# K transposed head by head: 8 transposes a step for 12, and copies that move between partition halves

## The chip, the cores and the metric

The kernel runs on one core of a Trainium2 chip. Its engines are TensorE (PE; its weight loads are listed as PEld), VectorE (DVE), ScalarE (ACT), GpSimd (POOL) and SyncE (SP), which here issues most DMAs. The metric is the device time of one execution in microseconds, the median of three runs.

## The reference

Linear attention with decay over blocks, and then a mixture of experts that takes for each token the two best of 8 by noisy gates. The change is in the first part, of which this is the core (4 batches, 8 heads, 768 positions, 64 channels):

```python
for b in range(nb):
    sl = slice(b * block, (b + 1) * block)
    qb, kb, vb = (q[:, :, sl], k[:, :, sl], v[:, :, sl])
    intra = np.einsum('bhic,bhjc->bhij', qb, kb) * Dmask[None]
    intra = np.einsum('bhij,bhjd->bhid', intra, vb)
    inter = np.einsum('bhid,bhde->bhie', qb * lam_pow[None], kv_state)
    out[:, :, sl] = intra + inter
    rev_pow = lam[:, None, None] ** (block - 1 - pos[None, :, None])
    kb_dec = kb * rev_pow[None]
    kv_state = lam_block[None, :, None, None] * kv_state + np.einsum('bhsd,bhse->bhde', kb_dec, vb)
```

The result, as 3072 tokens of 512 channels, goes through gates (`x @ w_gate` plus noise scaled by `log1p(exp(x @ w_noise))`) and, for each expert, `relu(x @ w1) @ w2`, weighted and added up.

## The kernel before

**Steps.** The attention is done in 12 steps of 256 positions each, numbered u (or t, with u = t + 1 in the loop). A chunk of 128 positions takes the place of the reference's block; its mask of powers, Mk, is built once at the start, sent through DRAM and loaded back. In a step the tile of K lies in SBUF as 128 partitions by head, x and channel: partition p holds positions 2p and 2p + 1, and x says which of the two.

**K transposed.** The scores need K with the channels on the partitions: kT is 128 partitions (two heads s of 64 channels) by 4 pairs of heads by 2 by 128. `trans_k` (L319) makes it with TensorE transposes, four to a PSUM bank (one for each pair of heads), and copies the bank to kT. Before, three banks are filled. In the first, a transpose takes x = 1 of one head and x = 0 of the next, which lie side by side, and one copy of 128 partitions moves the bank. In the other two, a transpose takes 128 columns of which only one half of the partitions is used, and a copy moves that half. So every copy stays on its own partitions, and the second index of kT is x for one head and 1 - x for the other; `scores` (L372) reads it as `x ^ s`. Where u is 0 the copies are on DVE (L332), else on ACT (L330).

**Order of a loop step.** Nothing schedules the work; each engine does what stands in the program, in that order. For PE a step (L981) is: K's transposes (`trans_k`, L328), the products for the state (`kv`, L419), Q's transposes (`trans_q`, L344), the sums over the chunk and over the state (`intra` and `inter`, L384), the transposes of the step before to token order (`store_x`, L450), its products with the gates (L438), the next scores (`scores`, L372), a part of `inter`, and the gates' sums (L466). DVE multiplies the scores by the mask (L375), updates the states (L428, L431), scales Q (L351), and does the gates' and the routing's arithmetic a few operations at a time, as `advance` hands them out.

**PSUM banks.** `bank()` (L313) takes the next of a pool of four banks; an allocation waits until the bank of the allocation four before it has been read. The banks pO, pKV, pL and pR are others. K and Q of step 1 are transposed in the prelude, before the loop, into pO, pKV and pL (L664, L665); a few dummy products (`keep_warm`, L177) stand around them.

**After the loop** come the experts, from L1046 on: products of 128 x 128 weights with the gathered tokens (L895, L933).

Of the kernel before, what the change touches and what calls it, by code (L numbers as in the profile page):

```python
# [26 lines left out]
AF = mybir.ActivationFunctionType  # L27
# [3 lines left out]
B, H, S, D = 4, 8, 768, 64  # L31
# [94 lines left out]
def kernel(  # L126
# [3 lines left out]
    nc = tc.nc  # L130
# [58 lines left out]
    identf = consts.tile([128, 128], FT, name="identf")  # L189
# [126 lines left out]
    def half(i):  # L316
        return slice(i * 64, (i + 1) * 64)

    def trans_k(u, banks=()):  # L319

        banks = iter(banks)
        kT[u] = aw.tile([128, HP, 2, C], FT, name="kT", bufs=1)
        flat = KT[u].rearrange("p h x d -> p (h x d)")
        for at, y, r in ((D, 1, slice(0, 128)), (0, 0, half(0)), (2 * D, 0, half(1))):
            nm = next(banks, None)
            p = psum.tile([128, HP, C], FT, name=nm) if nm else bank()
            for hp in range(HP):
                nc.tensor.transpose(p[:, hp, :], flat[:, hp * 4 * D + at:hp * 4 * D + at + 2 * D], identf)  # L328
            if u:
                nc.scalar.activation(kT[u][r, :, y, :], p[r], AF.Copy)  # L330
            else:
                nc.vector.tensor_copy(kT[u][r, :, y, :], p[r])  # L332

    def trans_q(u, banks=()):

# [26 lines left out]
    def scores(u):  # L362
        AT[u] = []
        for r in range(2):
            at = aw.tile([128, 2, 2, 2, C], FT, name="at")
            AT[u].append(at)
            ps = [bank().rearrange("p (h x) i -> p h x i", x=2) for _ in range(2)]
            for h in range(2):
                for x in range(2):
                    for s in range(2):  # L370
                        for a in range(2):
                            nc.tensor.matmul(ps[s][half(a), h, x, :], kT[u][half(s), 2 * r + h, x ^ s, half(a)],  # L372
                                             qT[u][half(s), 2 * r + h, a * C:(a + 1) * C], start=True, stop=True)
            for s in range(2):
                nc.vector.tensor_mul(at[:, s], ps[s], mask(s, slice(2 * r, 2 * r + 2), slice(0, C)))  # L375
# [285 lines left out]
    kdecay(0)  # L661
    load(2, "kt")
    load(2, "vt")
    trans_k(1, ("pO", "pKV", "pL"))  # L664
    trans_q(1, ("pO", "pKV"))  # L665
    keep_warm(WARM[1])
    kv(0)
    kdecay(1)
# [312 lines left out]
    for t in range(NST):  # L981
        u = t + 1
# [268 lines left out]
    with tc.For_i(0, n_over) as it:  # L1251
# [13 lines left out]
        r = rp.tile([128, 1], I32, name="reco")  # L1265
# [61 lines left out]
```

## Time and profile before

| | |
|---|---|
| median of three runs | 718.95 us (718.71 to 720.71) |
| span of the profiled execution | 716.8 us |
| its own time beside the span | not listed; the runs' median is 2.15 us above the span |
| PE busy | 698.8 us (97%) |
| DVE, ACT, POOL busy | 398.3, 223.3, 361.8 us |
| attention loop, t = 1 to 10 | 28.7 to 134.4 us |

The span runs from the first to the last instruction, the device time of a run also over what lies around that. A busy share is a mean over stages: DVE is busy for 56% of the span, but for over 90% of some steps of the loop. The rows of the chain of waits give a start, a duration, and the engine and line; the rows of a timeline give the same for one engine, with the idle time before it and what ended that in brackets.

### The profile page before, as it was taken

Reading aid. Unit: us, or ns where it says so; the run is one execution under the profiler, and the core shown is the slowest. Engines: PE = TensorE matmul, PEld = TensorE weight load, DVE = VectorE, ACT = ScalarE, POOL = GpSimd, SP = SyncE. Lnnn points to the kernel's source line nnn. Section 1 sums busy time; section 2 is a strip of 40 time slices with the busy share of each in tenths; the row PEclk is TensorE's granted clock in tenths of the full one; section 3 lists DMA queues with packets and bytes.
Section 4 is the critical chain, followed back from the end, with each engine's and each line's share of the span. In section 5 each row is a group of like instructions: output and inputs, shape, how many; then the busy total and the mean of one; then the engine's idle time right before and its main releaser. Section 6 shows DMA issues by size and latency. Waiting matters only on the chain.

```text
span 716.8 us, 15851 instructions
## 1 busy us (share of the span) xinstructions
PE 698.8 (97%) x6014; PEld 600.4 (84%) x6014; DVE 398.3 (56%) x1044; ACT 223.3 (31%) x382; POOL 361.8 (50%) x505
## 2 busy tenths in 40 slices
PE   7899999999999999999999999999999999999994
PEld 5888888889898898988888888888888898888883
DVE  4755899879355546743674367337624662565210
ACT  2255545542143312332233214222322242223100
POOL 4411342313453865687768567836773768321221
PEclk9999999999999999999999999999999999999998
DMA  9998986580645725273627352735452554330110
GB/s 203 263 230 245 251 232 203 188 305 25 180 131 168 207 56 179 82 185 87 183 93 176 85 186 84 176 88 161 116 154 79 170 143 122 104 116 30 51 51 32
DMA packets 94192, 104.32 MB, mean 146 GB/s; under 512 B 41234, under 2 KB 66844, under 8 KB 94112
## 3 DMA queue, kind: packets, MB, share of 16 engines
q1 hardware_dynamic: 79456, 65.73, 34.0%
q0 software_dynamic: 13552, 37.00, 17.0%
q10 hardware_dynamic: 1104, 0.53, 0.5%
q8 instruction: 49, 0.80, 0.5%
q14 instruction: 31, 0.25, 0.1%
HBM read 78.28 MB, written 26.12 MB: 146 GB/s over the span
## 4 chain that ended last, share of the span: by engine, by line
PE 89%; issue 4%; DMA 2%; POOL 1%; DVE 1%; ACTq 0%; SPq 0%; ACT 0%; POOLq 0%
PE pS L895 37%; PE pKV L933 16%; PE pO L933 16%; PE pO L384 3%; PE pS L372 3%; PE pS L328 2%; PE pS L450 2%; PE pO L938 2%; PE pS L419 2%; PE pS L344 1%; PE pKV L384 1%; PE pKV L938 1%; DMA Mk<-powd 1%; PE pR L438 1%; PE pS L874 1%
## 5 line engine op out<-in xcount | busy, mean ns | idle before, releaser
L839 POOL DMA_INDIRECT xg<-x_tok,recq x147 | 161.0, 1095 | 45.6 <-issue 40.0
L895 PE MATMUL pS<-xth,w1h 128*128 128x512 f32 (+3 forms) x544 | 181.4, 333 | 0.9 <-DVE ht L905 0.9
L895 PE MATMUL pS<-xth,w1l 128*128 128x512 f32 (+3 forms) x544 | 180.5, 332 | 0.0
L895 PE MATMUL pS<-xtl,w1h 128*128 128x512 f32 (+3 forms) x544 | 180.5, 332 | 0.0
L905 DVE SCALAR_TENSOR_TENSOR ht<-pS,ht 128x256 fp32r<-128x256 f32 (+3 forms) x176 | 75.8, 454 | 123.1 <-ACT ht L901 120.7
L933 PE MATMUL pKV<-w2h,ht 128*128 128x512 f32 x384 | 122.6, 390 | 0.0
L933 PE MATMUL pO<-w2h,ht 128*128 128x512 f32 x384 | 122.4, 390 | 0.0
L952 POOL DMA_INDIRECT out_dram<-ot,rec x46 | 60.7, 1319 | 121.0 <-DVE ot L945 110.8
L901 ACT ACTIVATE ht<-pS 128x512 fp32r<-128x512 f32 (+3 forms) x136 | 65.2, 483 | 173.2 <-PE pS L895 167.7
L895 PEld LDWEIGHTS pS<-xth,w1h 128*128 128x128 f32 x544 | 102.7, 189 | 10.4 <-DVE ht L905 1.1
L895 PEld LDWEIGHTS pS<-xth,w1l 128*128 128x128 f32 x544 | 102.7, 189 | 8.8
L895 PEld LDWEIGHTS pS<-xtl,w1h 128*128 128x128 f32 x544 | 102.7, 189 | 8.8
L933 PEld LDWEIGHTS pO<-w2h,ht 128*128 128x128 f32 x384 | 72.1, 188 | 14.9
L933 PEld LDWEIGHTS pKV<-w2h,ht 128*128 128x128 f32 x384 | 72.1, 188 | 14.9
L866 ACT ACTIVATE xth<-turned 128x512 fp32r<-128x512 f32 (+1 forms) x39 | 23.7, 607 | 167.5 <-DVE turned L864 167.5
L933 PE MATMUL pKV<-w2l,ht 128*128 128x512 f32 x192 | 74.9, 390 | 0.0
L933 PE MATMUL pO<-w2l,ht 128*128 128x512 f32 x192 | 74.8, 390 | 0.0
L360 POOL TENSOR_TENSOR kd<-kt,Mk 128x512 f32<-128x512 f32 x24 | 24.8, 1051 | 73.4 <-PE pR L419 51.6
L917 POOL DMA_INDIRECT pv<-out_dram,rec x46 | 47.0, 1021 | 14.2 <-issue 12.0
L375 DVE TENSOR_TENSOR at<-pS,Mk 128x512 f32<-128x512 f32 x48 | 29.9, 683 | 23.0 <-PE pS L372 18.5
L808 DVE TENSOR_TENSOR w2l<-wst,w2h 128x1024 fp32r<-128x1024 f32 (+1 forms) x33 | 39.2, 1191 | 6.1 <-ACT w2h L807 5.6
L933 PEld LDWEIGHTS pKV<-w2l,ht 128*128 128x128 f32 x192 | 36.1, 188 | 7.4
(241 smaller groups left out, 941.5 us busy)
## 6 DMA issues: line engine op xcount, KB each, us to landing
wst<-in_moe_w_dram SPq DMA_DIRECT2D x36, 512.0 KB, 4.2
wst<-in_moe_w_dram SPq DMA_DIRECT2D x96, 128.0 KB, 3.7
x_tok<-xc SPq DMA_DIRECT2D x24, 272.0 KB, 4.7
kt<-in_k_dram SPq DMA_DIRECT2D x12, 512.0 KB, 5.2
qt<-in_q_dram SPq DMA_DIRECT2D x24, 256.0 KB, 5.2
vt<-in_v_dram SPq DMA_DIRECT2D x12, 512.0 KB, 5.7
out_dram<-zero SPq DMA_DIRECT2D x24, 256.0 KB, 3.6
xg<-x_tok,recq POOLq DMA_INDIRECT x147, 2.8
```

The costliest lines, as they stand in the source:

```text
L360: nc.gpsimd.tensor_mul(kd[:, :, s], kt[:, :, s], mask(s, slice(0, HP), slice(C - 1, C)).to_broadcast([128, HP, 2, D]))
L375: nc.vector.tensor_mul(at[:, s], ps[s], mask(s, slice(2 * r, 2 * r + 2), slice(0, C)))
L384: nc.tensor.matmul(PO[u][a][half(g), hp, :], lhs, rhs, start=n == 1, stop=n == (8 if not (u % NW or a) else 12 if u else 10))
L808: nc.vector.tensor_tensor(lo[:, r], st[:, r], hi[:, r].bitcast(FT), op=SUB)
L839: nc.gpsimd.indirect_dma_start(out=XG[t][:, g * QW:(g + 1) * QW], out_offset=None, in_=x_tok.rearrange("t (q w) -> (t q) w", w=QW), in_off ...
L866: nc.scalar.activation(hi, raw, AF.Copy)
L895: nc.tensor.matmul(p, W1[a][d][:, fs], xt(b, cs)[:, d], start=(d == 0 and i == 0), stop=(d == DB - 1 and i == 2))
L901: nc.scalar.activation(ht(e, 0, f, cs), p, AF.Relu)
L905: nc.vector.scalar_tensor_tensor(ht(e, 1, f, c), p[:, r], 0.0, ht(e, 0, f, c).bitcast(FT), op0=OP.max, op1=SUB)
L917: nc.gpsimd.indirect_dma_start(out=PV[t][:size(e, t), :], out_offset=None, in_=out, in_offset=bass.IndirectOffsetOnAxis(ap=REC[e, t], axis=0),
L933: nc.tensor.matmul(p, ht(e, a, f, cs), W2[b][f // 2][:, f % 2, :], start=(i == 0), stop=(i == len(terms) - 1))
L952: st = nc.gpsimd.indirect_dma_start(out=out, out_offset=bass.IndirectOffsetOnAxis(ap=REC[e, t], axis=0), in_=o, in_offset=None, bounds_che ...
```

## The change

The transposes of K now take one head at a time: 128 columns, which are x = 0 and x = 1 of that head. So two banks hold all of K, 8 transposes a step and not 12. In a bank, partitions 0 to 63 are x = 0 and 64 to 127 are x = 1 of one head; they have to go to the half of kT that belongs to the head, so each bank is copied in two halves, and in two of the four copies source and target are different halves of the partitions. The index of kT is then plain x. In the prelude the banks are dealt out anew.

```diff
@@ trans_k @@
-        for at, y, r in ((D, 1, slice(0, 128)), (0, 0, half(0)), (2 * D, 0, half(1))):
+        for s in range(2):
             nm = next(banks, None)
             p = psum.tile([128, HP, C], FT, name=nm) if nm else bank()
             for hp in range(HP):
-                nc.tensor.transpose(p[:, hp, :], flat[:, hp * 4 * D + at:hp * 4 * D + at + 2 * D], identf)
-            if u:
-                nc.scalar.activation(kT[u][r, :, y, :], p[r], AF.Copy)
-            else:
-                nc.vector.tensor_copy(kT[u][r, :, y, :], p[r])
+                nc.tensor.transpose(p[:, hp, :], flat[:, (2 * hp + s) * 2 * D:(2 * hp + s + 1) * 2 * D], identf)
+            for x in range(2):
+                if u:
+                    nc.scalar.activation(kT[u][half(s), :, x, :], p[half(x)], AF.Copy)
+                else:
+                    nc.vector.tensor_copy(kT[u][half(s), :, x, :], p[half(x)])
@@ scores @@
-                            nc.tensor.matmul(ps[s][half(a), h, x, :], kT[u][half(s), 2 * r + h, x ^ s, half(a)],
+                            nc.tensor.matmul(ps[s][half(a), h, x, :], kT[u][half(s), 2 * r + h, x, half(a)],
@@ prelude @@
-    trans_k(1, ("pO", "pKV", "pL"))
-    trans_q(1, ("pO", "pKV"))
+    trans_k(1, ("pO", "pL"))
+    trans_q(1, ("pKV", "pO"))
```

Lines below `trans_k` are one higher after the change (L344 is L345, L372 is L373).

In the loop, PE's queue of the step t = 3 was as follows, from the last gates' sum of the step before to Q's transposes; the names after the arrow are the operands, numbers tell PSUM allocations apart, and the brackets say whose semaphores an instruction waits for:

```order
L466 MATMUL pL_742<-sel_166,xp_893 128x16
L328 MATMUL pS_949<-identf_94,kt_579 128x128 [waits DMAHW7_49,DVE_49]
L328 MATMUL pS_949<-identf_94,kt_579 128x128 x3
L328 MATMUL pS_955<-identf_94,kt_579 128x128 [waits DVE_49]
L328 MATMUL pS_955<-identf_94,kt_579 128x128 x3
L328 MATMUL pS_961<-identf_94,kt_579 128x128 [waits DVE_49]
L328 MATMUL pS_961<-identf_94,kt_579 128x128 x3
L419 MATMUL pS_969<-vt_656,kd_808 64x64 [waits DMAHW2_49,DVE_49,Pool_49]
...
L344 MATMUL pS_1016<-identf_94,qt_621 128x128 [waits DMAHW0_49,Activation_49]
L344 MATMUL pS_1016<-identf_94,qt_621 128x128 x3
L344 MATMUL pS_1023<-identf_94,qt_621 128x128 [waits DMAHW1_49,Activation_49]
```

The same place after the change:

```order
L467 MATMUL pL_730<-sel_166,xp_877 128x16
L328 MATMUL pS_933<-identf_94,kt_567 128x128 [waits DMAHW7_49,DVE_49]
L328 MATMUL pS_933<-identf_94,kt_567 128x128 x3
L328 MATMUL pS_940<-identf_94,kt_567 128x128 [waits DVE_49]
L328 MATMUL pS_940<-identf_94,kt_567 128x128 x3
L420 MATMUL pS_949<-vt_644,kd_792 64x64 [waits DMAHW2_49,DVE_49,Pool_49]
...
L345 MATMUL pS_996<-identf_94,qt_609 128x128 [waits DMAHW0_49,DVE_49]
L345 MATMUL pS_996<-identf_94,qt_609 128x128 x3
L345 MATMUL pS_1003<-identf_94,qt_609 128x128 [waits DMAHW1_49,PE_49,Activation_49]
```

The third bank of K (pS_961) is gone with its wait; Q's first bank waits for DVE in place of ACT, and its second for ACT and for PE's own earlier work.

ACT's queue in the same step before, with kT and qT as the targets of the copies and xo that of the sums' copies:

```order
L330 ACTIVATE kT_948<-pS_949 128x4x128
L330 ACTIVATE kT_948<-pS_955 64x4x128
L330 ACTIVATE kT_948<-pS_961 64x4x128
L347 ACTIVATE qT_1014<-pS_1016 128x4x128
L347 ACTIVATE qT_1014<-pS_1023 128x4x128
L406 ACTIVATE xo_1071<-pO_937 128x512
```

And after:

```order
L331 ACTIVATE kT_932<-pS_933 64x4x128 x2
L331 ACTIVATE kT_932<-pS_940 64x4x128 x2
L348 ACTIVATE qT_994<-pS_996 128x4x128
L348 ACTIVATE qT_994<-pS_1003 128x4x128
L407 ACTIVATE xo_1051<-pO_921 128x512
```

Each bank of K is now emptied by two copies, four in all, ahead of the same copies of Q.

## Rows read from the trace of the kernel before

**Rows 1.** Page, first section: busy us (share of the span) and instructions.
```profile
PE 698.8 (97%) x6014; PEld 600.4 (84%) x6014; DVE 398.3 (56%) x1044; ACT 223.3 (31%) x382; POOL 361.8 (50%) x505
```

**Rows 2.** Chain that ended last, in order of time: start us, us, what.
```profile
60.20 1.36 PE pS L328 x12
61.56 1.08 PE pS L419 x32
...
67.60 1.91 PE pS L372 x64
...
70.49 1.36 PE pS L328 x12
...
123.19 1.85 PE pS L328 x12
...
139.64 1.63 PE pS L895 x12
```

**Rows 3.** Busy time by step of the loop (a step's bounds, its length, the engines).
```profile
70.50:80.80 10.30, 10.30 (x258) 8.98 (x258) 9.27 (x38) 5.09 (x10) 2.09 (x2) 1.00 0.90 254
...
112.80:123.20 10.40, 10.36 (x259) 8.94 (x257) 9.57 (x43) 6.19 (x11) 4.27 (x4) 1.00 0.47 145
```

**Rows 4.** Timeline of PE's weight loads, 91 to 95 us: start us, us, operation, [idle before].
```profile
91.36 1.29 PEld L328 LDWEIGHTS pS<-identf,kt 128*128 128x128 f32 x12
92.82 1.01 PEld L419 LDWEIGHTS pS<-vt,kd 64*64 64x64 f32 x32 [0.17 <-issue]
93.90 0.86 PEld L344 LDWEIGHTS pS<-identf,qt 128*128 128x128 f32 x8
94.92 0.14 PEld L384 LDWEIGHTS pO<-at,vt 64*64 64x64 f32 x2 [0.17 <-issue]
```

**Rows 5.** Timeline of ACT, 60 to 65 us; the second row is part of the first.
```profile
60.78 1.69 ACT L330 ACTIVATE kT<-pS 128x512 f32<-128x512 f32 x3 [1.69 <-PE pS L328]
...
61.28 1.20 ACT L330 ACTIVATE kT<-pS 64x512 f32<-64x512 f32 x2
...
63.32 1.09 ACT L347 ACTIVATE qT<-pS 128x512 f32<-128x512 f32 x2 [0.85 <-PE pS L344]
```

**Rows 6.** L941: duration ns min/median/max, first and last start.
```profile
L941 ACT ACTIVATE pv<-pO x1: 594/594/594, 223.5 to 223.5; 64x512 f32<-64x512 f32 x1
```

**Rows 7.** Timelines of DVE and of PE's weight loads, 110 to 133 us.
```profile
110.47 2.48 DVE L375 TENSOR_TENSOR at<-pS,Mk 128x512 f32<-128x512 f32 x4 [0.72 <-PE pS L372]
...
122.46 2.46 DVE L375 TENSOR_TENSOR at<-pS,Mk 128x512 f32<-128x512 f32 x4
...
123.78 0.42 PEld L328 LDWEIGHTS pS<-identf,kt 128*128 128x128 f32 x4 [0.18 <-DVE at L375]
124.38 0.42 PEld L328 LDWEIGHTS pS<-identf,kt 128*128 128x128 f32 x4 [0.18 <-DVE at L375]
...
132.20 2.48 DVE L375 TENSOR_TENSOR at<-pS,Mk 128x512 f32<-128x512 f32 x4 [1.60 <-PE pS L372]
```

**Rows 8.** The prelude: DVE, the chain, ACT, PE's weight loads.
```profile
8.92 0.69 DVE L332 COPY kT<-pS 64x512 f32<-64x512 f32 x1
...
10.12 7.05 DMA Mk<-powd
...
16.60 0.60 ACT L347 ACTIVATE qT<-pKV 128x512 f32<-128x512 f32 x1 [0.31 <-PE pKV L344]
...
18.41 0.13 PEld L419 LDWEIGHTS pS<-vt,kd 64*64 64x64 f32 x1 [1.29 <-POOL kd L360]
```

**Rows 9.** Busy time by stretch: PE, PEld, DVE, ACT, POOL, granted clock, DMA.
```profile
9.00:10.00 1.00, 0.32 (x3) 0.08 (x1) 0.97 (x2) 0.00 (x0) 0.00 (x0) 1.00 1.24 263
...
17.00:18.00 1.00, 0.25 (x2) 0.12 (x2) 0.71 (x2) 0.19 (x1) 0.70 (x1) 1.00 1.37 227
...
19.00:22.00 3.00, 3.00 (x83) 3.00 (x79) 1.94 (x7) 0.00 (x0) 1.70 (x2) 0.50 1.04 266
```

**Rows 10.** Loads of kt: time from issue to landing.
```profile
DMA to landing us min/median/max: 4.4/5.2/5.5
```

## Prediction

> **What bounds the kernel now.** I read the page's first section and then the chain of waits. TensorE is busy 698.8 of 716.8 us [rows 1], so the only gains to be had are PE time itself or its few waits. The chain, in order of time, says where the changed lines lie on it: in the attention loop every block of PE work follows the last one without a gap. The step that begins at 60.20 is: 12 transposes of K (L328, 1.36 us), the states' products (L419, 1.08), later the scores at 67.60, and at 70.49 the next step's 12 transposes [rows 2]. There are ten such steps (t = 1 to 10, the last at 123.19), 10.5 us each on the mean of the six from 60.20 on, and in all of them L328 is on the chain. The other two calls, K of steps 0 and 1, lie in the prelude, before 15 us, where the chain runs through something else: the mask's DMA (10.12 for 7.05 us), after which GpSimd scales K and PE, idle for 1.29 us, starts at 18.41 [rows 8].
>
> Who is next behind PE? The table by step has the answer: ACT is busy 5 to 6 us of a step, but DVE 9.27 of 10.30 and 9.57 of 10.40 in steps that carry the routing [rows 3]. So one engine has slack and the other hardly any. The loads of K land 4.4 to 5.5 us after issue [rows 10] and are issued two steps, some 20 us, before their transposes. They are not what PE waits for, and stay so with steps 4% shorter.
>
> **The change, part by part.**
>
> *Four transposes less a step.* From the first weight load of L328 to that of the next line there are 1.46 us for 12 transposes (91.36 to 92.82); L344 makes 8 of the same shape with the same hand-over in 1.02 us (93.90 to 94.92). The weight loads alone are 1.29 and 0.86 [rows 4]. The difference is 0.43 to 0.44. Bounds: 1.36 by the chain less 1.02 gives 0.34; 4/12 of 1.36 gives 0.45 [rows 2]. I take 0.43, the weight loads' own, since nothing else on PE changes: 10 x 0.43 = 4.3 us (3.4 to 4.5). The 4 transposes of each call in the prelude count for nothing, as above.
> Against so much speaks a figure of the Trainium skill, "TensorE: Matmul & The Clock Gate", section "Back-to-back issue gap": a sustained stream of weight loads and matmuls of 128 columns has some 81 ns for each. By it 40 transposes would be worth an estimated 3.2 us, the sum below would be lower by 1.1 and the time 716.2. This case's trace does not agree: 1.29 us for 12 of these fp32 transposes are 107 ns each [rows 4], and the trace's figure stands.
>
> *Four copies for three on ACT.* The copies are 64 partitions high and as long as before in the free dimension; a copy of 64 partitions takes as long as one of 128 (0.59 to 0.60). The cost beside this is in the spacing. Three copies take 1.69 us from 60.78; the last two take 1.20 of it from 61.28, end to end, so the second starts 0.50 after the first and the third 0.60 after the second, and there the partition half changes [rows 5]. Now the half changes, on the reading or the writing side, at every copy. So 4 x 0.60 = 2.40 us a step against 1.69 [rows 5].
> The first copy starts 0.58 after the step's start on the chain, the fourth ends at 2.98. The copy of Q's first half started 3.12 after it (63.32), and PE now brings that half 0.43 sooner, at 2.69. It waits 0.3 us, behind the copies of K. The copies of Q then end near 4.1, and the scores, which need them, come at 7.0 (67.60 less 60.20 less 0.43). Cost 0, under 2.9 us of cover. ACT's sum rises by 0.71 a step to at most 7 of 10: not a bound.
>
> *Half the copies cross the partitions.* The trace has one such copy already, L941, which moves rows 64 to 127 of a bank to rows 0 to 63: 594 ns [rows 6], like any other. Taken as 0.60.
>
> *PSUM banks.* The pool has four, and an allocation waits for the release of the one four before it. The order in a step was k0 k1 k2, state, q0 q1, then two of `store_x` and four of the scores; k2 is now missing. Who waits for whom moves by one: the state product now waits for the third mask multiply (L375) of the step before and not the fourth; q0 for the fourth, instead of for k0's copy; q1 for both of k0's copies. These end at 0.58 + 1.20 = 1.78, and PE comes to q1 at 0.92 + 1.08 + 0.51 = 2.5. Cover 0.7 us, cost 0. An extra semaphore on q1 costs between 0 and one transpose's slot (0.11), 0 to 1.1 us in ten steps; I take 0, since PE's sequencer runs ahead of it.
>
> *DVE is late in two places.* In the step of 112.80 it has hardly any idle time (9.57 busy of 10.40) [rows 3]; the four multiplies at its end start at 122.46 [rows 7], and PE waits for them: its groups of four transposes stand at 123.19, 123.78 and 124.38, not 0.43 apart, and the block takes 1.85 us in place of 1.36 [rows 2]. PE now reaches that point 0.43 sooner and DVE doesn't. The first two groups start where they did, and the state product can go at about 124.4, for 125.0 before. So two steps together save 0.6 and not 0.86: 0.26 lost. For the other step as full, that of 70.50 [rows 3], I estimate 0.1 lost. At 132.20 DVE waits 1.60 us for PE again [rows 7], so this debt is paid there and nothing of it reaches the experts. Sum of losses 0.35, with bounds 0 and, if every step from 70 us on were as tight, 6 x 0.43 = 2.6.
>
> *The prelude.* On DVE four copies for three, +0.69 us [rows 8]; the scores of step 0 start that much later, at about 11.1. On ACT the copies of Q, the last of which started at 16.60, end about 0.8 later, at 18.0. All of it lies under the mask's DMA and the product at 18.41 that follows from it [rows 8], and the first accumulation into the banks that these copies empty stands behind that product. Cost 0, under 0.4 us of cover and more; without it up to 0.8.
>
> *The experts* (from 140 us on) run the same instructions. They start when PE gets there and shift as a whole.
>
> Sum: 4.3 - 0.35 = 3.95, say 3.9 us. On the profiled execution 716.8 becomes 712.9 of span. The median of the runs is 718.95, 2.15 above the span, which holds what lies around it and what executions differ by. I carry the difference over: 718.95 - 3.9 = 715.1 us.
>
> **The rivals.**
>
> *DVE becomes the bound.* For it: 9.57 of 10.40 us busy, and the waits at 123.78 and 124.38. Against it: in the other steps the four multiplies start just after the scores that feed them, and the idle 0.72 before 110.47 [rows 7] is more than 0.43. If all steps from 70 us on gain nothing, four steps are left: 4 x 0.43 = 1.7, 717.2 us.
>
> *The clock.* Between 19 and 22 us PE ran at a granted clock of 0.50, that is at 1.2 GHz and not 2.4, after it had been busy for only 0.25 of the us from 17 to 18; over these 3 us it cost 1.5 [rows 9]. The change makes another hole wider: PE was busy 0.32 of the us from 9 to 10 [rows 9], and now its transposes end 0.43 sooner and the scores start 0.69 later. If the clock falls there as well, the scores and transposes that follow stretch into the hole before 18.41. Two outcomes: the later fall is spared, since PE was busier before it, and 1.5 more is gained (713.6); or a second one lands on the path, 716.6. The Trainium skill, "TensorE: Matmul & The Clock Gate", section "Part 4: PE-mode transpose", says that transposes don't count as busy like other matmuls. By that rule only the later scores matter, not the missing transposes. No row here shows transposes alone, so I leave both outcomes in.
>
> *Slower: the crossing copy is dear.* The point from which it decides is q1's bank. With 0.7 us of cover a crossing copy of more than 1.3 us makes PE wait in every step. For 2.2 us slower than before, PE must lose 6.5 us, 0.65 a step, so that copy must take 1.95 us: 721.2. Against it stands L941 at 594 ns [rows 6]. DVE shows no crossing copy from PSUM, but there it is hidden.
>
> *Nothing gained.* If PE's transposes had been hidden behind something the chain doesn't show, the time stays at 719. Only the DMA engines (busy all through the first steps) could be that, and no row has PE waiting for them in the loop.
>
> **How the numbers follow.** About 0.3% (2.2 us) is what a measurement of this kernel can tell from no change. Forecast (3.0 to 4.5 gained): 0.70. Clock in favour, 713.6: 0.08; clock against, 716.6, just inside faster: 0.06. DVE bound, 717.2: 0.09, which counts as the same. Nothing gained: 0.04. Slower: 0.03. The likeliest case alone has 714.4 to 716.0; down to 713.3 and up to 717.9 the range takes in the clock's two outcomes and DVE as the bound, and leaves out some 1 in 10. Faster: 0.70 + 0.08 + 0.06 = 0.84, less 0.01 for spread at the edge: 0.83. Same: 0.14. Slower: 0.03.
>
> **What would show it right or wrong.** In the chain of the changed kernel, L328 with 8 transposes near 0.92 us a step, and the steps shorter by 0.43; the scores of the last step, and with them the first expert product (139.64 before [rows 2]), about 4 us sooner. ACT with four copies about 0.60 apart, Q's copy right behind the fourth. PE's waits for DVE at L375 no longer than 0.6 us in the step near 119. Wrong would be: weight loads of q1 waiting for ACT in every step (the crossing copy), waits for L375 in most steps from 70 us on (DVE), or a granted clock of 0.50 in other stretches than 19 to 22 us.

## The result, and the profile after

The changed kernel takes 724.19 us (median of 5 runs, 721.49 to 724.66), the kernel before 718.9 beside it: ratio 1.0054, 95% interval 1.0036 to 1.0071. The forecast was 715.1. So the change costs 0.5% where it was to gain 0.5%. The profiled execution of after spans 719.7 us (716.8 before). It is the fastest of the five (721.49), so its profile holds 2.9 us of a loss that is 5.3 us by the medians; the profile of e5 below, the same kernel in an execution of 724.59 us, holds more. The whole difference of the two profiles is there when the experts begin: their first product starts at 142.51 us in place of 139.64 [rows 2], and what is left of the span is 577.2 us in both.

The chain of waits of after, in order of time (start us, us, what):

```profile
5.22 6.79 DMA vt<-in_v_dram
12.03 0.58 ACTq L207
...
60.34 0.92 PE pS L328 x8
61.26 1.08 PE pS L420 x32
62.34 1.02 PE pS L345 x8
...
126.66 1.25 PE pS L328 x8
...
142.51 1.63 PE pS L896 x12
```

The eight transposes take 0.92 us, for 1.36 [rows 2]: the saving is there. Two things are new. The chain of the prelude runs through the load of v and ScalarE's fourth issue of the mask (L207), where it ran through the mask's own transfers [rows 8]; and the K block at 126.66 stretches over waits.

ScalarE's timeline (start us, us, operation, [idle before]) is what the prediction said, four copies 0.60 apart and Q's right behind them (before: [rows 5]):

```profile
60.92 2.42 ACT L331 ACTIVATE kT<-pS 64x512 f32<-64x512 f32 x4 [2.01 <-PE pS L328]
63.37 1.09 ACT L348 ACTIVATE qT<-pS 128x512 f32<-128x512 f32 x2
```

The starts of the K blocks (first weight load of L328 in PE's timeline) give the loop step by step. Lengths in us from the block near 60 us (before 59.94, after 60.08) to the first weight load of the experts; the last two columns are experiments told below, one without GpSimd's scaling of K, one with that scaling later:

| from K block | before | after | no scaling (e3) | scaling later (e13) |
|---|---|---|---|---|
| 60 | 10.29 | 9.85 | 9.85 | 9.85 |
| 70 | 10.29 | 11.36 | 9.94 | 10.55 |
| 81 | 10.84 | 11.91 | 10.44 | 11.41 |
| 92 | 10.46 | 10.02 | 10.02 | 10.02 |
| 102 | 10.85 | 11.07 | 10.41 | 11.35 |
| 113 | 10.52 | 12.37 | 11.16 | 10.60 |
| 124 to the experts | 16.38 | 15.78 | 15.66 | 15.79 |
| sum | 79.63 | 82.36 | 77.48 | 79.57 |

Three steps of after (60, 92 and 124) are 0.44 to 0.60 shorter, where 0.43 was predicted. The four others are longer than before. What PE waited for between 28 and 145 us (waited for, us in total, times, longest):

```profile
PE pS L328 <- DVE at L376: 3.1, 2, 1.8
PE pR L420 <- issue: 2.1, 1, 2.1
```

The first row is two stops in the loop, 1.25 us until 81.29 and 1.84 until 126.66. The second lies ahead of it, at 28.47; what PE waits for there is found further below. So VectorE's mask products (`at` in the rows) come late twice. The prediction had allowed for at most 0.6 us in one place, and had named waits in most steps as the sign that VectorE is the bound. Why are they late? A routing step below is one VectorE operation of the gates' and the routing's arithmetic, such as L101. VectorE's and GpSimd's timelines of after at the first two places where such steps are longer:

```profile
72.29 0.19 DVE L118 TENSOR_SCALAR arena<-arena 128x64 f32<-128x64 f32 x1
72.52 2.02 DVE L101 SCALAR_TENSOR_TENSOR arena<-arena 128x64 f32<-128x64 f32 x2
74.46 0.41 DVE L429 COPY S<-pS 128x256 f32<-128x256 f32 x1
...
80.56 1.87 DVE L376 TENSOR_TENSOR at<-pS,Mk 128x512 f32<-128x512 f32 x3
...
72.40 2.06 POOL L361 TENSOR_TENSOR kd<-kt,Mk 128x512 f32<-128x512 f32 x2 [7.85 <-PE pR L420]
...
105.54 1.13 DVE L622 TENSOR_SCALAR hb<-hb,rowf 128x224 bf16<-128x224 bf16 x1
106.59 1.16 DVE L625 TENSOR_SCALAR hb<-hb 128x112 bf16<-128x112 bf16 x2
...
105.55 2.06 POOL L361 TENSOR_TENSOR kd<-kt,Mk 128x512 f32<-128x512 f32 x2 [3.87 <-PE pR L420]
```

And the same place of the kernel before:

```profile
72.82 0.49 DVE L101 SCALAR_TENSOR_TENSOR arena<-arena 128x64 f32<-128x64 f32 x2
73.22 0.42 DVE L428 COPY S<-pS 128x256 f32<-128x256 f32 x1
...
73.13 1.08 POOL L360 TENSOR_TENSOR kd<-kt,Mk 128x512 f32<-128x512 f32 x1 [8.29 <-PE pR L419]
```

Read the starts. GpSimd's scaling of K (`kdecay`) waits for PE to finish the states' product, which reads the old scaled K. Before, that came at 73.13, 2.90 us after the K block's start, when VectorE was ending its last routing steps, and VectorE went on to the state update, whose operations read PSUM. Now it comes 2.47 us after the start, that is 0.43 sooner. Two routing steps of VectorE are still to come, with all their operands in SBUF, and each takes 1.0 us in place of 0.24: it ends when one of GpSimd's two instructions of 1.05 us ends. The same at 105.5 and at 116.7 (again two L101 in 2.10). The Trainium skill, "SBUF — State Buffer", section "Who interferes with whom", has this as a rule: VectorE and GpSimd share a pair of SBUF ports, and whichever takes it first keeps it for the whole instruction. The trace agrees: each of the two L101 lasts until one GpSimd instruction is over.

The wait at 80 us has a second cost. The windows of after around it (length, PE, PEld, DVE, ACT, POOL, granted clock, DMA share, GB/s):

```profile
80.00:81.00 1.00, 0.04 (x1) 0.00 (x0) 0.93 (x4) 0.00 (x0) 0.00 (x0) 1.00 1.08 334
81.00:82.00 1.00, 0.71 (x5) 0.53 (x6) 1.00 (x3) 0.00 (x0) 0.00 (x0) 0.94 0.99 309
82.00:83.00 1.00, 1.00 (x8) 0.67 (x10) 1.00 (x3) 0.94 (x2) 0.00 (x0) 0.50 0.35 88
```

PE stood still for 1.25 us and then ran at a granted clock of 0.50, that is 1.2 GHz, for some 3 us more. e5 gives the price of that: its step from 82 us has the same late block without the low clock and takes 10.49 us, 1.4 less than the 11.91 of after.

### The profile page after: what moved, and what is told of

The parts are those of the page before. It is cut to its first block, busy times and chain, and to the rows that moved or that the text cites. A ratio compares the mean times of both kernels' runs of the same rounds, so it can differ in the third digit from the quotient of the medians.

```text
span 719.7 us, 15774 instructions
## 1 busy us (share of the span) xinstructions
PE 697.8 (97%) x5966; PEld 597.8 (83%) x5966; DVE 403.6 (56%) x1045; ACT 231.0 (32%) x393; POOL 361.0 (50%) x505
## 4 chain that ended last, share of the span: by engine, by line
PE 84%; DVE 6%; issue 5%; DMA 2%; POOL 1%; SPq 1%; ACT 0%; ACTq 0%; POOLq 0%; DVEq 0%
PE pS L896 37%; PE pKV L934 16%; PE pO L934 16%; PE pO L385 2%; PE pS L373 2%; PE pO L939 2%; PE pS L420 1%; PE pS L328 1%; DVE at L376 1%; PE pS L451 1%; PE pS L345 1%; PE pKV L939 1%; DMA vt<-in_v_dram 1%; DVE arena L101 1%; PE pS L875 1%
## 5 line engine op out<-in xcount | busy, mean ns | idle before, releaser
L934 PEld LDWEIGHTS pO<-w2l,ht 128*128 128x128 f32 x192 | 36.0, 188 | 7.4
```

The lines of the kernel that those rows point to most:

```text
L934: nc.tensor.matmul(p, ht(e, a, f, cs), W2[b][f // 2][:, f % 2, :], start=(i == 0), stop=(i == len(terms) - 1))
```

## The experiments

The runs are told in groups. They were made on several chips; before takes 719.2 us on two of them (e5 to e8, e12 to e15) and 732 to 740 on the others, where its times also scatter by over 1%. Every ratio is against before on the same chip.

**The changed kernel again (e5).** No edit.

> The changed kernel once more, beside the kernel before and the three kernels that follow, all on one chip. Both theories are about the loop and the prelude: (1) the fourth DMA of the mask waits on ScalarE's queue until the first vt load has landed, and GpSimd's scaling of K stands on VectorE's SBUF-only routing steps in the K blocks of about 72, 105 and 117 us (single steps of 1.0 us in place of 0.23 to 0.28). Expected again: the four issues of L207 take 4.2 to 4.6 us together, a first K block of the loop at 30 to 31 us, K blocks 11 to 12.5 us apart after these three, ratio to before 1.002 to 1.008. (2) rival: what was seen was one execution's accident (loads that came late): then the issues take 2.6 to 2.9 us here, no K block is over 10.9 us without a late load, and the ratio is 0.994 to 0.998.

1.0057 (1.0036 to 1.0078). Issues of L207 4.50 us; long steps after 71 (11.34), 103 (11.62) and 115 us (12.23), and the experts begin at 145.44. Here the low clock follows the second stop (1.84 us, until 126.82), and it lasts longer (columns as above):

```profile
127.00:133.00 6.00, 6.00 (x56) 5.22 (x60) 4.70 (x18) 3.33 (x6) 1.99 (x9) 0.50 0.03 11
133.00:134.00 1.00, 1.00 (x34) 1.00 (x32) 0.90 (x4) 0.22 (x1) 0.74 (x4) 0.72 0.00 0
```

From that block to the experts e5 needs 18.63 us and after 15.78, so 2.85 us of this execution's loss are the clock behind the stop. The loss is no accident of one execution, but how much of it is the clock differs from one to the next.

**The mask in the prelude (e1, e2, e15).** ScalarE issues the mask in four DMAs. Each waits for a completion semaphore shared with an earlier DMA, and the change moved the fourth onto another one. The instruction order of before, then of after:

```
L207 DMA Mk<-powd 64x4x128 [waits DMAHW4_49]
L207 DMA Mk<-powd 64x4x128 [waits DMAHW5_49]
```

The one was the second load of k, which has landed by then; the other is the load of v that the chain shows landing at 12.01. The four issues take 4.45 us and not 2.64, and PE's first product of states starts at 20.3 (18.41 in [rows 8]), the loop at 30.60 and not 28.65. In e1 and e15, one kernel on two chips, step 0 alone is as before:

```diff
+        if u == 0:
+            for at, y, r in ((D, 1, slice(0, 128)), (0, 0, half(0)), (2 * D, 0, half(1))):
...
+            return
```

and in e2 steps 0 and 1 are as changed and the loop as before (`if u > 1`).

> Changed kernel, with step 0's K alone transposed in the old way (three copies on DVE). Then the fourth DMA of the mask waits for the load of kt again and not for that of vt. Theory (that wait costs the prelude): the fourth issue ends before 11 us and not at 12.6, the mask lands near 17.2 and not 19.5, the loop's first L328 starts near 28.8 and not 30.7, and the time is about 1.9 us under the changed kernel's (722.3 for 724.2), the loop itself being as long as in the changed kernel. Rival (the prelude is later because PE's clock fell between 13 and 20 us, whatever the DMA): the loop still starts near 30.5 and the time stays near 724.

> Changed kernel in steps 0 and 1, kernel before in the steps of the loop. Theory: the prelude keeps its loss and the loop loses nothing, so the loop starts near 30.6, its ten steps are as long as before (105.7 us), and the time is 718.9 + 1.9 = 720.8. Rival (the loss is all in the loop): 718.9. Rival (the prelude costs more in the usual run than in the profiled one): 722 or more.

> The same kernel as in the run e1_step0_old (step 0 with the old twelve transposes, all else as changed), on the chip of the three kernels before it: what the mask's wait alone is worth in the time. Theory (two separate losses): the four issues of L207 2.6 to 2.8 us together, K blocks of the loop still 11.3 to 12.4 us apart after 70, 82 or 105 and 115 us, ratio 1.001 to 1.004. Rival (all of the late start is taken up before 60 us): as the changed kernel, 1.004 to 1.008. Second rival (the mask is the whole loss): 0.994 to 0.998.

e1: 1.0012 (0.9974 to 1.0049); e15: 1.0064 (1.0035 to 1.0094), issues 2.65 us, loop from 27.95. e2: 0.9992 (0.9960 to 1.0025), with 4.36 us of issues and the loop from 30.73. So the late mask is undone by e15 and the loss stays whole, as its first rival said, and e2 has the late mask and shows no loss, as its first rival said, not 1.9 us of it. It is real in the trace and costs nothing that can be told at the end: in the profiles of chips where before takes 719 us the loop starts anywhere from 27.52 to 30.98 us, and the K block near 60 us comes at 59.94 to 61.64 in all ten profiles (with before and after). Who starts sooner is held up on the way (below).

**No scaling of K (e3).** As e1, and GpSimd's scaling is left out from step 2 on, the old scaled K being used again. The later states are made of the old scaled K, so the routing sends other numbers of tokens to the experts, and only the loop is read.

```diff
+        if u >= 2:
+            KD[u] = KD[1]
+            return
```

> As the first, and GpSimd's scaling of K is left out from step 2 on (the states use step 1's scaled K, so the values and with them the tokens of each expert differ; only the loop is read). Theory (GpSimd's scaling starts 0.4 to 0.7 us sooner, while DVE is still in operations that read and write SBUF alone, and these wait for it): no such DVE operation takes over 0.4 us in the loop, PE waits less than 0.6 us in all for L375's multiplies, and from the loop's first L328 to the first expert product there are about 4 us less than before (106.6 to 107.2 for 110.9). Rival (DVE has too much work whatever GpSimd does): PE still waits 1 to 2 us in two steps, 109 to 111 us. Rival (the four copies on ACT hold up what follows): the same 109 to 111, with PE waiting for ACT.

The step table has it: 77.48 us from the block near 60, 2.15 less than before, 4.88 less than after (1.4 of them the clock). From the loop's first block to the experts it takes 108.78 us, 110.92 before and 106.6 to 107.2 expected: half of what was hoped for. PE has no wait of 0.15 us or more for a mask product. e3 keeps ScalarE's four copies and the same VectorE operations, so neither of the two by itself is the loss. L101 between 60 and 145 us (busy, mean ns | idle before) in after:

```profile
L101 DVE SCALAR_TENSOR_TENSOR arena<-arena 128x64 f32<-128x64 f32 x14 | 6.3, 449 | 0.4
```

The same row of e3:

```profile
L101 DVE SCALAR_TENSOR_TENSOR arena<-arena 128x64 f32<-128x64 f32 x14 | 3.1, 224 | 0.4
```

Without a partner on GpSimd, the same 14 instructions take half the time.

**The same meeting in the kernel before (e8).** If the loss is where the two engines meet, the kernel before must lose too when half a microsecond more of VectorE's routing stands ahead of the state update. `FILL` is the work, in estimated us, that `advance` hands out in a step before the next state update, `FILLS` that behind Q's scaling.

```diff
-FILL, SPLIT, FILLS = 2.0, 1.2, 3.4
+FILL, SPLIT, FILLS = 2.5, 1.2, 2.9
```

> The kernel before with FILL 2.5 and FILLS 2.9: half a microsecond more of VectorE's routing work ahead of each state update, about what the change takes away of TensorE's time ahead of it. Nothing of the transposes, of PE's work or of VectorE's total is changed. Theory (K scaling on GpSimd that starts while VectorE is in steps with SBUF operands alone makes each of these take about 1 us): collisions appear in two or three K blocks (L101, L514 to L517, L584 to L593, L612), each costs 0.7 to 1.6 us of VectorE, and at least two at-products come late: ratio 1.002 to 1.006, the stretch from the loop's first K block to the first expert product 112.3 to 114.5 us in place of 110.9. Rival (VectorE's total decides, or its backlog is taken up in the same step): ratio 0.999 to 1.001.

1.0037 (1.0024 to 1.0049). The timeline at the place shown above:

```profile
72.92 2.49 DVE L101 SCALAR_TENSOR_TENSOR arena<-arena 128x64 f32<-128x64 f32 x4
75.33 0.41 DVE L428 COPY S<-pS 128x256 f32<-128x256 f32 x1
...
73.23 2.09 POOL L360 TENSOR_TENSOR kd<-kt,Mk 128x512 f32<-128x512 f32 x2 [8.28 <-PE pR L419]
```

Four steps take 2.49 us, where 14 take 3.1 in e3. Between 60 us and the experts, six VectorE operations of e8 take over 0.25 us more than the same ones of e3, 4.5 us in all; in after they are six with 4.9 us, in e5 six with 5.0, in the kernel before one with 0.7 (a cast at 83.62 us, 0.93). No transpose was touched. This shows that the position of VectorE's work against the scaling by itself makes the kernel before slower by 0.37%, for the 0.54 to 0.57% of the change. The profiled execution is the slowest of e8's eight (725.0 us) and overshoots what was expected: 116.84 us from the loop's first block to the experts, with a low clock of some 7 us behind its late block at 126.48.

**Less routing ahead of the state update (e4, e6, e9, control e7).** As e1, with FILL, FILLS 1.2, 4.2 (e4, e6) or 1.5, 3.9 (e9); e7 is the kernel before with 1.2, 4.2.

```diff
-FILL, SPLIT, FILLS = 2.0, 1.2, 3.4
+FILL, SPLIT, FILLS = 1.2, 1.2, 4.2
```

> As the first, and 0.8 us of the routing's arithmetic a step is handed out after Q's scaling and not before the state's update (FILL 1.2 for 2.0, FILLS 4.2 for 3.4), so that DVE is at the state's update, which reads PSUM, when GpSimd starts. Theory: DVE's stalls of about 1 us go, DVE is no longer late, PE keeps most of its 4.3 us, 714.5 to 715.5. Rival (DVE has too much work): the multiplies are as late as without it, 718 or more.

> The changed kernel with the old twelve transposes in step 0 alone (so that the mask's fourth DMA does not wait) and VectorE's routing work shared out otherwise: FILL 1.2 in place of 2.0 before the state update, FILLS 4.2 in place of 3.4 after it. The same kernel as in the run e4_fill, now on the chip of the changed kernel's own run. Theory (the two waits are the loss): ratio to before 0.993 to 0.998, that to the changed kernel 0.988 to 0.994, with no routing step of VectorE of 0.9 us or more beside a K scaling on GpSimd, and the full 0.43 us per K block showing in the steps. Rival (VectorE as a whole is the bound once PE is faster): the same VectorE work only stands elsewhere, the at-products come as late, and the ratio is 1.000 to 1.004.

> As the run e6_new_fill, but with FILL 1.5 and FILLS 3.9, half a microsecond and not 0.8 of routing work moved behind the state update; about what the change takes off TensorE's time ahead of it. Theory (the loss is GpSimd's K scaling on VectorE's SBUF-only steps, and 1.2 moved more than the collision needs): still no routing step of 0.9 us beside a K scaling, and the at-products that came 0.7 us late with 1.2 come in time: the stretch from the K block near 60 us to the first expert product 78.5 to 79.6 us (79.93 with 1.2, 82.4 to 84.2 in the changed kernel, 79.63 in the kernel before), ratio to before 0.9965 to 0.999. Rival (VectorE's total in these steps is the bound, wherever it stands): 79.8 to 80.5 us, ratio 0.999 to 1.001.

> The kernel before with FILL 1.2 and FILLS 4.2, nothing else changed: the control. Theory (the shift cures collisions that the change brought): the kernel before has a single one (a 0.93 us CAST at 83.6 us), so -0.9 to +0.9 us, ratio 0.9988 to 1.0012. Rival (the new shares are better whatever the transposes): ratio 0.994 to 0.997, as much as the changed kernel gained by it.

e4: 0.9961 (0.9926 to 0.9995); e6: 0.9992 (0.9978 to 1.0006); e9: 0.9986 (0.9952 to 1.0021); e7: 1.0015 (1.0004 to 1.0027), a little over what was expected. In e4, e6 and e9 no VectorE operation from 60 us on is lengthened any more (L101 is back at 225 ns in e6 and e9), and by the ratios e6 is 0.65% under the changed kernel on the same chip. But from the block near 60 it needs 79.93 us, not less than before: routing that stands behind the state update makes the mask products late (1.2 us in two places in e6). e6 lies between its theory and its rival. A gain showed on e4's chip only, and e9's 80.51 us for the stretch speaks for its rival. With equal shares of routing the new transposes win by 0.23% (e6 against e7, whose intervals just overlap).

**The scaling later (e12, e13, control e14).** One instruction: GpSimd first reads a column of the new state, and so starts the scaling when VectorE has begun the update. Shares are as in the changed kernel. e12 has step 0 as before, e13 is the changed kernel, e14 the kernel before.

```diff
             state(u)
+            nc.gpsimd.tensor_copy(seen, SA[u, 1][:, 0, :1])
             kdecay(t + 2)
```

> The changed kernel with step 0 as before (no late mask) and one instruction more per step: GpSimd copies one column of the state that VectorE has just written, ahead of its scaling of K, so that the scaling starts behind the state update and not when TensorE has read the old scaled K. Shares of routing work as in the changed kernel (FILL 2.0). Theory (where the two engines meet is the loss in the loop): the routing steps ahead of the state update take 0.19 to 0.28 us each again; the stretch from the K block near 60 us to the first expert product 77.3 to 78.8 us (82.4 and 84.2 in the changed kernel, 79.6 in the kernel before); ratio to before 0.9955 to 0.998. Rival (VectorE's work in the steps of 70 to 125 us, with ScalarE's fourth copy ahead of its qTs products, is itself the bound, so that TensorE's 0.43 us can't be had there): 79.4 to 80.6 us, ratio 0.999 to 1.001. Second rival (the scaling, now later, stands on the routing steps behind the state update): single steps of about 1 us behind qTs, over 80.6 us, ratio over 1.001.

> The changed kernel as it is, with that one instruction of GpSimd alone. Theory (two separate losses): the loop as in e12_gate, the prelude as in the changed kernel with the fourth mask DMA waiting (issues of L207 4.2 to 4.6 us together): ratio 0.9985 to 1.001, 1.5 to 2.5 us above e12_gate and 2.5 to 5 us under the changed kernel. Rival: the late start of the loop is taken up again before 60 us by steps of 9.85 us, so the same time as e12_gate within 0.7 us.

> The kernel before with that one instruction: the control. Its K scaling starts within 0.3 us of the state update anyway, but for the step of 83 us. Theory: -0.9 to +0.4 us, ratio 0.9988 to 1.0006. Were the ratio 0.9955 to 0.998 here too, the gain of e12_gate would not speak of the change.

e12: 0.9999 (0.9984 to 1.0013); e13: 1.0001 (0.9990 to 1.0012); e14: 1.0015 (1.0006 to 1.0024). Timeline of e13:

```profile
72.91 0.48 DVE L101 SCALAR_TENSOR_TENSOR arena<-arena 128x64 f32<-128x64 f32 x2
73.31 0.42 DVE L429 COPY S<-pS 128x256 f32<-128x256 f32 x1
...
75.32 0.83 DVE L101 SCALAR_TENSOR_TENSOR arena<-arena 128x64 f32<-128x64 f32 x1
...
73.86 0.18 POOL L993 COPY seen<-S 128x1 f32<-128x1 f32 x1 [8.42 <-DVE S L429]
74.00 2.06 POOL L361 TENSOR_TENSOR kd<-kt,Mk 128x512 f32<-128x512 f32 x2
```

One instruction takes the changed kernel from 1.0057 (e5) to 1.0001, some 4 us, and on one chip from 1.0064 (e15) to 0.9999 (e12, which is e15 with that instruction): the meeting, with the late mask products and the low clock that follow from it, is the loss. It isn't free: the scaling now reaches one step behind the update (0.83 for 0.23, one of two operations still lengthened, 0.9 us in all), and in the kernel before, which hardly had the meeting, the instruction costs 1.1 us (0.0015). e12 and e13 are equal, which settles the mask too: my theory of two separate losses (e13 1.5 to 2.5 us above e12) was wrong, its rival right. And neither is faster than before: e12's first rival had the time and the stretch (80.37 us), but VectorE is not all of it, as PE's gaps show next. By the ratios e13 is 0.14% faster than e14, which has the instruction too.

**Where the rest of the gain is (e10, control e11).** PE has gaps in most of the new kernels for which the waits name no cause; the value products have no semaphore to wait for at all. PE's timeline of e12, within runs of scores and value products:

```profile
49.05 0.92 PE L384 MATMUL pS<-qT,kT 64*64 64x128 f32 x25 [0.46 <-issue]
54.82 0.33 PE L396 MATMUL pO<-at,vt 64*64 64x128 f32 x2 [0.49 <-issue]
...
109.03 0.33 PE L396 MATMUL pO<-at,vt 64*64 64x128 f32 x2 [1.81 <-issue]
```

In e6 the first two stand at the same instructions (47.70 and 53.48); PE of before is idle for 0.08 us from 30 to 60, and after has one such gap in the loop, 0.24 us at 108. The DMA engines are full from 30 to 60 (share 1.01 in after, 1.06 in e6, 0.97 before), so two loads of the experts' weights, 1 MB, were taken out of e6's kernel (e10) and of before (e11); GpSimd fills the tiles with a constant in their place.

```diff
+        if (which, j) in ((1, 0), (1, 1)) and not e:
+            nc.gpsimd.memset(st, 0.03)
...
```

> As the run e6_new_fill, without the first two loads of the experts' weights (1 MB in the loop's first two steps; GpSimd fills the two tiles with a constant, so the output is not the reference's; the work behind is the same). Theory (the loop's first steps are held by the DMA engines, share about 1.0 from 8 to 60 us, so that every kernel so far has its K block near 60 us at 59.9 to 61.3 whatever it saved before): with 1 MB less, at 250 to 280 GB/s 3.7 to 4.2 us of transfers, TensorE's gaps of 0.5 us after 36, 47 and 53 us go, the three K blocks are 9.8 to 10.1 us apart and the one near 60 comes at 57.0 to 58.3 us; ratio to before 0.9955 to 0.998. Rival (the gaps belong to the code, not to the transfers): it comes at 59.9 to 60.6 us, ratio 0.999 to 1.000.

> The kernel before without the same two loads (a constant in their place, so the output is not the reference's): the control for the run e10_new_nowload. Both theories of that run expect little: TensorE of the kernel before is busy without a break from 30 to 60 us, its K blocks are 10.3 to 10.55 us apart, and fewer transfers can give at most what its prelude waits for. K block near 60 at 59.4 to 60.1 us, ratio 0.999 to 1.0005. Were the gain as large as that of the changed kernel (0.9955 to 0.998), the loads would have been in both kernels' way alike and would not say where the change's saving went.

e10: 0.9900 (0.9854 to 0.9946); e11: 1.0010 (0.9973 to 1.0046). That suggests that the loads are in the new kernel's way and not in the old one's. The profiles don't show it: on that chip e9, which has the loads (and FILL 1.5), also runs its early steps at 9.77 to 9.86 us without a gap, and all three have the K block at 58.3 to 58.6 (e10's profiled execution is the slowest of its six).

What PE waits for in these gaps can be read from the traces. A DMA queue that the profile names `instruction` brings packets of 16,384 bytes, one for every 256 of PE's matmuls, weight loads and sequencer instructions. Its row in the page of e12, and in the DMA view of e12 from 106.6 to 107.6 us, ahead of the gap that ends at 109.03:

```profile
q8 instruction: 48, 0.79, 0.5%
...
q8 instruction: 1, 0.02, 5.8%
```

Leaving aside e16 and e17, where the states' product has waits of its own (below), the profiles have 52 gaps without a releaser from 20 us to the experts, 0.18 to 2.1 us long. All 52 stand at the same place of a period of 256 instructions, within one instruction, and in all PE goes on 1.2 to 1.7 us after a packet of that queue has landed (at 107.57 in the example). So PE waits for its next instructions, also at 28.47 in after. No run changed this, and why a packet comes late, whether for the full DMA engines or not, stays open.

**Q before K (e16, control e17).** The transposes of Q ahead of those of K should move the scaling behind the routing and free VectorE of ScalarE's fourth copy.

```diff
         if t and u < NST:
+            trans_q(u)
+            load(t + 3, "qt")
             trans_k(u)
...
-            trans_q(u)
```

> The changed kernel with another order in the loop's step: the transposes of Q (and their copies, and VectorE's qTs products) ahead of those of K, and the load of the next Q with them; every operation is the same. The product of v and scaled K then ends 1.02 us later after the step's first transpose, so GpSimd's scaling of K starts that much later, when VectorE is in qTs and the state update, both of which read PSUM; and the qTs products no longer wait for ScalarE's four copies of K. Theory (loss: where the two engines meet; missing gain: VectorE's chain from qTs to the at-products, with ScalarE's fourth copy in front of it): no routing step of 0.9 us beside a scaling, at-products in time, the stretch from the K block near 60 us to the first expert product 76.8 to 78.6 us (79.6 before, 82.4 and 84.2 changed), ratio 0.994 to 0.998. Rival (VectorE's sum of work in these steps is the bound whatever stands ahead of it): 79.3 to 80.3 us, ratio 0.999 to 1.001, as with the later scaling in e13_after_gate. Second rival (gaps of TensorE that the profile shows no cause for take the rest): no late at-product, but two or more gaps of 0.5 to 1 us, 78.5 to 80 us, 0.998 to 1.000.

> The kernel before with the same order, Q ahead of K: the control. TensorE of the kernel before is busy without a break in the loop, and its scaling already meets the state update, so theory: ratio 0.9985 to 1.001. If it is 0.994 to 0.998 too, the order is a gain of its own and e16_new_qfirst is to be read against this run: the transposes saved are then worth the difference of the two, 2.5 to 4.3 us by the theory, 0 to 1 us by the rival.

e16: 1.0037 (0.9997 to 1.0077); e17: 1.0045 (1.0010 to 1.0081). A miss for every theory. The meeting is not gone (five operations are lengthened in each, 2.6 us in all in e16 and 3.4 in e17), and PE's waits of e16 show another loss:

```profile
PE pS L420 <- issue: 4.6, 5, 1.4
```

The states' product now stands still in seven steps: the five of the row, and two (1.7 and 1.1 us) that the profile puts down to GpSimd operations which had ended 0.2 and 0.5 us before. Its bank of PSUM comes four allocations after Q's first, which VectorE frees in a qTs product that stands behind the routing. The trace agrees: in six of the seven the product starts 0.1 us after a qTs product has ended (52.60 and 52.70, for instance). VectorE no longer waits for qT (0.0 us), and it brought nothing.

No version that does all the work beats the kernel before for certain: of their intervals e4's alone lies below 1, and the same kernel on the quieter chip, e6, does not bear it out.

## Why the prediction was wrong

**Right.** Four transposes are worth 0.43 to 0.44 (steps of 9.85 for 10.29). ScalarE's copies are 0.60 apart and Q's stands behind them. A copy across partitions costs no more than another. No K block of the loop waits for ScalarE's bank: in PE's waits of after from 28 to 145 us L331 doesn't occur. The experts shift as a whole.

**The step that failed: "DVE is late in two places", loss 0.35.** I asked whether VectorE would be ready 0.43 us sooner. I did not ask whom PE's earlier finish would release: GpSimd's scaling, off the chain and on an engine that is idle for most of a step, moved onto VectorE's SBUF-only steps. Late mask products cost PE 3.1 us in the profile and not 0.35, and the low clock behind the first one came on top (1.4 us; 2.85 in e5, behind the second); the stretch from 60 us lost 2.73 where 7 x 0.44 = 3.1 were to be gained. The sign comes from this: e8 makes it without the change, e3 and e13 take it away. Of the rivals only "Slower" had the sign, by a crossing copy that makes PE wait; the copies are 0.60 apart, so that was not it. The windows from the block near 60 us to the experts give PE's part (length, PE, PEld, DVE, ACT, POOL, granted clock, DMA share, GB/s). Before:

```profile
59.94:139.57 79.63, 79.59 (x1879) 69.04 (x1878) 66.67 (x240) 42.32 (x79) 25.93 (x60) 1.00 0.77 226
```

After:

```profile
60.08:142.44 82.36, 78.97 (x1851) 67.67 (x1850) 70.29 (x240) 47.21 (x86) 26.09 (x60) 0.98 0.76 219
```

And e13:

```profile
60.46:140.03 79.57, 77.94 (x1852) 66.55 (x1851) 66.85 (x240) 47.20 (x86) 27.78 (x67) 1.00 0.81 228
```

VectorE is busy 70.29 us for 66.67 with the same 240 instructions: 3.6 us are spent blocked. PE is idle 0.04, 3.39 and 1.63 us.

**"Six steps as tight as that" was the better bound, but not because VectorE has too much work.** In e3, with all of VectorE's operations and no scaling beside them, five of the six steps from 60 to 124 us are 0.35 to 0.44 us shorter than before; the sixth, from 113, has a PE gap of 0.67 us for instructions. The stretch gains 2.15 of the 3.1. Where the scaling stays, other things take the gain up. In e13 the step from 70 (10.55) ends with mask products that come late behind the lengthened operation at 75 us, that from 113 (10.60) with a wait of 0.56 us for VectorE without any lengthened operation, and in those from 81 and 102 PE waits 0.48 and 0.51 us for instructions. By the number the rival "Nothing gained" (719, chance 0.04) comes nearest to what the change is worth once the meeting is all but gone (e13 719.24, e6 719.06), but that is luck: its mechanism, transposes hidden behind something else, is not what the steps of 9.85 us show. "DVE becomes the bound" (717.2, chance 0.09) is too low and has the cause in part. In e6 VectorE also waits 2.9 us for ScalarE's copies of Q between 60 and 145 us, 1.1 before: ScalarE's fourth copy costs nothing only while VectorE is held up by something else.

**"The prelude: cost 0" was wrong in the trace and right in the time.** I looked at what the copies delay, not at the DMA issue whose semaphore the new order of DMAs changes: the loop starts 1.95 us later. What I also missed is that these profiles don't pass an earlier start on to 60 us: in after the three steps before that make up for the late start and no more, and in e12 and e6, which start sooner, PE waits 1.4 us there for instructions. So three of the ten steps brought nothing at the end, 3 x 0.43 = 1.3 us of the sum.

**The clock.** The rival saw a second low stretch, but in the prelude. There PE does run at 0.50 for longer (0.54 on the mean of 13 to 20 us); it costs as little as the mask does, for e13's profile has no low clock there and its loop starts no sooner (30.98, after 30.60). The stretch that counts came after VectorE's lateness.

## What to carry to other kernels

When a change brings an engine sooner to a point, list everything that this point releases, on engines far from the chain too, and look in the trace at what VectorE does at that very time: a GpSimd operation that starts half a microsecond sooner can cost more than the half microsecond saved. Count a saving only in stretches whose ends move with it: a stretch that other starts don't shift at its end (here the first 60 us) takes it up. And test a suspected collision by moving it into the kernel that hasn't got it; that told more here than taking it out of the one that has. Where an engine stands without a releaser, set the packets of the instruction queue beside the gap.

## What was not expected of the hardware

- A VectorE instruction of 0.2 to 0.3 us with SBUF operands takes 0.9 to 1.1 us when GpSimd's tensor operation of 1.05 us has just started ahead of it; VectorE's operations on PSUM beside the same GpSimd operation keep their 0.41 and 0.86 us.
- A DMA's issue can wait on its own queue for the landing of an unrelated, earlier load (here 1.8 us longer than before, until 12.03 us), and a change of other instructions can switch that wait on.
- PE stood 0.2 to 1.8 us in the middle of the loop's matmuls for its next instructions: but for e16 and e17, all such gaps fall on one place of every 256 instructions, and PE goes on 1.2 to 1.7 us after a packet of the instruction queue.
- The same kernel ran at a granted clock of 0.50 behind another of its two late blocks, and twice as long, in another execution (3.4 us from 81.9 in after, 6.8 us from 126.7 in e5).
